# A new order of the same operations in a bucketed attention and token-mixing kernel

## The chip, the cores and the metric

The kernel runs on one core of one Trainium2 chip. The metric is the device time of one execution in microseconds; several executions are timed and the median is given. The core has five engines that take instructions in order, each from its own list: TensorE (PE, matrix products), VectorE (DVE), ScalarE (ACT, functions by tables), GpSimd (POOL), and SyncE (SP), which here issues the DMAs. They wait for one another by semaphores.

## The reference

Two parts follow each other for each of four batches. The first is attention with 8 heads, 768 positions and 64 dimensions, in which a query sees only the keys with the same six sign bits; the second works on the heads' outputs laid side by side (768 x 512).

```python
q_bits, k_bits = (q @ proj > 0), (k @ proj > 0)          # 6 bits, one bucket number each
mask   = q_bucket[:, :, :, None] == k_bucket[:, :, None, :]
scores = np.where(mask, scale * q @ k.T, -1e9)
attn   = exp(scores - max) / sum                         # per row
x      = (attn @ v) laid out as (B, S, H * D)

theta  = x @ w_theta                                     # 768x512 by 512x512
zr, zi = x * cos(theta), x * sin(theta)
u      = x + w_tok_r @ zr + w_tok_i @ zi                 # token mixing, 768x768 weights
out    = u + maximum(u @ w_ch, 0)
```

## The kernel before

**Attention, per head.** q and k are split into a high and a low 16-bit part (`hl`, L573 and L577), their sign bits are computed by a small product (`pb`, L627) and written beside them into the stacked operands `qt` and `kt` (copies of L646, else DMAs). A product `sq` gives scores from which DVE takes row maxima (`mc`, L721); these become a row of `qt`. Then the score product `st` is made again, transposed and with the maximum in it, ACT takes the exponential (`pf`, L799), ACT rounds it to 16 bits (`p1`, L805), POOL computes the rest (`p2`, L811; the profile shows both as `p`), and PE multiplies both with the split values (`po`, `pv` in the list), twice 65 and 64 columns. `vsc` and `vv` (L359 to L362, L490) scale and split the values. A normalisation (L849, L855) writes x.

**The second part, per batch and tile of 128 positions.** A transpose `pt_x` is split into `h_x` (ACT, L905) and `l_x` (DVE, L909); twelve matmuls make `ps_th` (one "theta tile"); ACT and DVE bring the angle to whole turns (`n` L941, `z` L944, its magnitude L950 on ACT or L947 on DVE). For tiles 0 to 2 together, and for 3 to 5, ACT takes sine and cosine (L966, L967), which need another table than exp: a table load stands ahead of them, and another ahead of the next `pf`. DVE makes `f` = x times sine or cosine (L978), which is split into a high half `zh` (L983 on ACT, L985 on DVE) and a low half `zl` (L989, POOL or DVE). Token mixing `py` is 36 matmuls for each output tile; then `u` (DVE, L1017), a transpose `pt_u`, `h_u`, `l_u`, twelve matmuls `ps_r`, `fin` (L1024) and the store. Batch b's second part is interleaved with batch b + 1's attention.

**What sets the order.** All of this is written as a list of operations: `op(name, prio, {engine: (planned duration, function)}, deps, slots, table)`. `prio` is a rank in steps of the attention (96 over the whole kernel) plus constants: `KA` and `KB` for rounding and rest, `PF` for the exponential, `TH0` and `TH1` for theta, `Y0`, `YS`, `Y1` for the mixing, `AS0` for assembling the operands, with variants for the first and last batch (`TH0_3`). `issue_all` runs a plan with planned durations: whenever an engine is free it issues the available operation of the lowest rank, held up by constants (`AHEAD`, `HOLD`, `PEN`, `WIN`). Operations with two engines go to the one that is free first by the plan. The result is a fixed list for each engine; nothing is reordered on the chip. Banks of PSUM come in three pools (`mx` 2, `s` 2 for `st`, `m` 4 for all others), and the matmuls go through a helper, so that all of them show as L78.

Of the kernel before, what the change touches and what calls it, by code (L numbers as in the profile page):

```python
# [34 lines left out]
def lsh_attention_moe_kernel(ctx: ExitStack, tc: tile.TileContext, q, k, v, proj, w_theta, w_tok_r, w_tok_i, w_ch, aff, out):  # L35
# [36 lines left out]
    pst = {}  # L72
# [24 lines left out]

    class Op:
        def __init__(self, name, prio, alts, deps=(), slots=(), table=None):
            self.name, self.prio, self.alts = name, prio, alts  # L100
            self.deps = [d for d in deps if d is not None]
            self.slots, self.table = list(slots), table
            self.phase = phase
            for sl in self.slots:
                sl.users += 1
            ops.append(self)

    ops = []
    phase = "0"
# [5 lines left out]
    def issue_all():  # L115
# [68 lines left out]
        def key(o, e):  # L184
            if e == "PE" and tail_pe in SHORT and o.name in FOUR:
                return (o.key[0] + PEN, o.key[1])
            return o.key
# [28 lines left out]
        while todo:  # L216
            progress = False
            for e in START:
# [3 lines left out]
                for o in avail[e]:  # L222
                    k_ = key(o, e)
                    if best is not None and k_ >= best:
                        continue
                    end = now + (HOLD * o.alts[e][0] if e != "SP" else 0)
                    if any(x.at < end and key(x, e)[0] + AHEAD < k_[0] for x in soon[e]):
                        continue
# [81 lines left out]
    def on(e, dur, fn):  # L310
        return {e: (dur, fn)}
# [28 lines left out]

    cload = op("consts", QKL + 0.03, on("SP", [(625, 0)] * 3, load_consts))
    proj_ready = op("pst", QK0, on("DVE", 700, split_proj), [cload])


    wth = [wp.tile([P, NC, DM], F32R, name=f"wth{i}") for i in range(2)]
# [108 lines left out]
    def prep_v(b, hp, prio):  # L454
# [62 lines left out]

        r = op("vload", prio + LV0, on("SP", [(450, 2 * S * D * 4)], load), slots=[svb])
        r = op("vsq", prio, on("ACT", 900, squares), [r], [svb, sv])
# [27 lines left out]
    def prep_qk(b, hp, G, g):  # L547
# [4 lines left out]
        ssc = t["ssc"] = Slot("sc")  # L552
        pr = G + at("QK0", b)
        for i, src in enumerate((q, k)):
            def part(i=i, src=src):
# [22 lines left out]

                a = op("qkload", G + QKL + 0.02 * i, on("SP", [(625, 2 * S * D * 4)], load), slots=[sn])
                raws.append(a)  # L580
# [25 lines left out]
        for i, sn, high, low in parts:  # L606
            hs.append(op("qkh", pr + QKI * i, pick(g, QKH, {"ACT": (830, high("ACT")), "DVE": (520, high("DVE"))}), [r], [sn, sh, ssc]))
            ls.append(op("qkl", pr + QKI * i, on("DVE", 880, low), [hs[-1]], [sn, sh, ssc]))

# [20 lines left out]

        b1 = op("bits", G + at("QK1", b), on("PE", 1000, bits), raws + [proj_ready], [sm_] + nats)
        direct = []
        if g == 0:
            direct.append(op("sign0", G + at("QK1", b) - 0.01, on("DVE", 4 * 470, first), [b1], [sm_]))
        fs = [op("sign", G + at("QK1", b), on("DVE", 570, sign), [b1], [sm_, sr])]

# [24 lines left out]
    def assemble(j, n_, t, prio, free_after):  # L661
# [12 lines left out]
        def bits():  # L674
# [8 lines left out]
            op("assemble", prio, on("SP", [(1000, 4 * D * n)] * 2 + [(1000, 2 * hd * n)] * 4, parts), t["parts"] + free_after, [sh]),  # L683
            op("assbits", prio + AB, on("SP", [(780, NM * n / 2)] * 4, bits), t["bits"] + free_after, [sr]),
        ]
# [8 lines left out]
    def maxima(h, n_, b, G, asm):  # L694
# [15 lines left out]
        for n, (parts, cs) in enumerate(units):  # L710
            def one(n=n, parts=parts, cs=cs):
# [10 lines left out]

                pr = G + at("MX0", b) + at("MX1", b) * n * T / len(units)
                a = op("qmax", pr, on("PE", 225, scores), asm, [sx])
# [26 lines left out]

        pr = G + at("MX0", b) + at("MX1", b) * T
        a = op("vboth", pr, on("DVE", 90, both), vs, [smc])
# [11 lines left out]
    def step(g, b, h, blk, mxt, vt, piece):  # L765
# [15 lines left out]
        for c in range(nc_):  # L781
            def chunk(c=c):
# [43 lines left out]

                G = g + CL * c * ni / 2
                a = op("st", G, on("PE", 440 + 8 * kc, scores), [mxt["rowd"]], [ss])
                last[n_].append(a)
                i = op("pf", G + PF, on("ACT", 490, pf), [a], [ss, spf], table="exp")  # L830
                d = [done] if done else [mxt["ftd"]] + vt["ready"]
                f = [sft] if c == 0 else []
                k1 = op("p1", G + KA, pick(g, P1, {"ACT": (525, p1("ACT")), "DVE": (337, p1("DVE"))}), [i], [spf, sp1])
                k2 = op("p2", G + KB, pick(g, P2, {"DVE": (610, p2(DVE)), "POOL": (1090, p2(POOL))}), [k1], [spf, sp1, sp2])
                return op("pv", G + KV, on("PE", 385 + 29 * ni * (c == 0), pv), d + [k1, k2], [sp1, sp2, sm_, vt["slot"], sx] + f)

            done = chunk()

        g += (nc_ - 1) * CL * ni / 2
        t["done"] = done  # L840
# [15 lines left out]

        r = op("recip", g + KN, on("DVE", 90, recip), [done], [sm_])
        n = op("norm", g + KN, on("DVE", 135 + 67 * n_, norm), [r], [sm_, sx])
        for i in range(*piece):
# [3 lines left out]
    def moe(b, G):  # L863
# [13 lines left out]

        st0 = op("moe", G + at("TH0", b) - 0.5, on("DVE", 800, start), wready["tk"] + vready[b], sz)

# [52 lines left out]
        for tt in range(T):  # L932
            def theta(tt=tt):
                prio = G + at("TH0", b) + at("TH1", b) * tt
                u, deps, sxt = transposed(lambda: tl[b][:, tt], f"x{b}_{tt}", prio, xready[b][tt // 2], "x")
# [99 lines left out]
    for tau in range(T):  # L1035
        prep_wtok(tau, W0 + WS * tau if tau < LATE else WL0 + WLS * (tau - LATE))
    for c in range(NC):
        split_weight(w_theta, wth, c, (0, DM), "th", "z0", "x", WTH + WTS * c, 1.0 / TWO_PI)
        for half in range(2):
            split_weight(w_ch, wch, c, (half * DM // 2, DM // 2), "ch", "tmp", "tmp", WC + WCS * (c + 0.5 * half))  # L1040
    g = 0
    for b in range(B):
        phase = str(b)
        for hp in range(NP):
            t = prep_qk(b, hp, g, g)
            vt = prep_v(b, hp, g + at("PV0", b))
            order = ORDERS[ORD if b == B - 1 and hp == NP - 1 else 0]
            mxs = []
            for j in range(2):
                n = ((b * NP + hp) * 2 + j) % SETS  # L1050
                free_after, last[n] = last[n], []
                G = g + sum(BLOCKS[k_][1] // 2 for _, k_ in order[: order.index((j, 0))])
                asm = t["first"] if g == 0 and j == 0 else assemble(j, n, t, G + at("AS0", b), free_after)
                mxs.append(maxima(2 * hp + j, n, b, G, asm))
# [3 lines left out]
    for b in range(B):  # L1058
        phase = str(b)
# [7 lines left out]
PSUM = (("mx", 2), ("s", 2), ("m", 4))  # L1067
BUFS = dict(mx=2, s=2, m=4, pf=4, p1=4, p2=4, vb=1, tmp=3)
SETS = 3
CL = 0.331  # L1070
TAIL = ["m", "s"]
ORDERS = [[(0, 0), (0, 1), (1, 0), (1, 1)], [(0, 0), (1, 0), (0, 1), (1, 1)]]
WIN = {"m": 3, "tmp": 3}
MX0 = -3.317
MX1 = 0.379
PIECES = [{1: (0, 3)}, {0: (0, 2), 1: (2, 3)}]
PF = 0.221
KA = 0.466
KB = 0.534
KV = 0.599  # L1080
KN = 1.56
AB = 0.161
WTH = 18.77
WTS = -0.673
WC = 23.047
WCS = 3.231
P1 = [(0, 999, ["ACT"])]
P2 = [(0, 999, ["POOL"])]
GR = 0
PEN = 0.031  # L1090
GR1 = 0
GROUPS = [[(0, 3), (3, 6)], [(0, 4), (4, 6)], [(0, 2), (2, 4), (4, 6)]]
JIT = 0
SEED = 162248
TH0_3 = -0.965
TH1_3 = 0.664
Y0_3 = 2.914
YS_3 = -0.142
Y1_3 = -0.008
MX0_0 = -3.169  # L1100
MX1_0 = 0.368
AS0_0 = -6.248
PV0_0 = -5.09
QK0_0 = -9.684
QK1_0 = -4.644
HOLD = 0.017
LATE = 6
WL0 = 26.724
WLS = -14.449
TH0_0 = 0.111  # L1110
TH1_0 = 0.797
Y0_0 = 9.844
Y1_0 = 1.882
YS_0 = 6.922
AHEAD = 1.647
QKL = -12.399
QKI = 4.506
QKH = [(0, 999, ["ACT", "DVE"])]
QK0 = -6.21
QK1 = -5.177  # L1120
AS0 = 0.585
PV0 = -4.184
LV0 = -2.609
W0 = -0.514
WS = 3.329
TH0 = -0.152
TH1 = 0.823
Y0 = 9.151
YS = 5.605
Y1 = 2.733  # L1130

_INS = ["q", "k", "v", "proj", "moe_w_theta", "moe_w_tok_r", "moe_w_tok_i", "moe_w_ch"]

# [44 lines left out]
```

## Time and profile before

| | |
|---|---|
| runs | 805.57, 806.96, 808.13 us; median 806.96 |
| profiled execution | 808.25 us, of which the span of the trace is 806.1 |
| mean granted clock of TensorE | 0.972 |
| PE, DVE, ACT, POOL busy | 732.8, 547.6, 552.1, 473.9 us |
| `po` (pv), all forms | 154.7 us in 3456 matmuls |
| `py` | 218.2 us in 864 matmuls |

A row of a page's group or a timeline reads: start, busy time, engine, line, operation, output and inputs (partitions x elements, type), count, and in brackets the idle time of the engine ahead of it with what ended it. Slices are fortieths of the span, about 20.15 us each; a digit is the busy share in tenths, and 9 is 90% or more.

### The profile page before, as it was taken

To read this page: it belongs to the slowest core of one execution; us is meant where nothing else is said; L and a number is where in the kernel's file an instruction comes from. 1 tells how busy PE (TensorE), PEld (TensorE's weight loads), DVE (VectorE), ACT (ScalarE), POOL (GpSimd) and SP (SyncE) were. 2 spreads that over 40 slices of the span, in tenths; PEclk is the share of its full clock that TensorE was granted. 3 is DMA by queue.
4 is the path that set the end of the run, shared out by engine and by line. 5 is a ranking of instruction groups with operands and counts; after the bars stand their busy time and mean duration, and the time that the engine had idled before them with its cause. 6 is when DMAs were issued, how large, how long until landed. Compare 5 with 4: busy or idle time off the path is not lost.

```text
span 806.1 us, 17749 instructions
## 1 busy us (share of the span) xinstructions
PE 732.8 (91%) x6760; PEld 472.2 (59%) x6760; DVE 547.6 (68%) x1027; ACT 552.1 (68%) x983; POOL 473.9 (59%) x496
## 2 busy tenths in 40 slices
PE   2578697779899999999899999999899999999998
PEld 1246465447555656767556666668556666675456
DVE  7989999895688746685786655684696755236413
ACT  5488899888787754898887564778796654657101
POOL 4168889687659724695569653765667564631200
PEclk9988999999899999999899999999899999999999
DMA  7354454433103232323003220332004110000002
GB/s 219 87 152 145 135 160 143 130 88 84 38 15 109 66 98 66 98 74 88 27 21 103 80 70 29 101 84 69 21 21 115 46 47 14 15 14 1 1 1 78
DMA packets 35268, 59.52 MB, mean 74 GB/s; under 512 B 7456, under 2 KB 24944, under 8 KB 35184
## 3 DMA queue, kind: packets, MB, share of 16 engines
q1 hardware_dynamic: 35184, 58.40, 25.3%
q8 instruction: 53, 0.87, 0.5%
q14 instruction: 31, 0.25, 0.1%
HBM read 32.51 MB, written 6.29 MB: 48 GB/s over the span
## 4 chain that ended last, share of the span: by engine, by line
PE 69%; DVE 13%; ACT 7%; issue 3%; POOL 3%; DMA 3%; SPq 1%; ACTq 0%; DVEq 0%; POOLq 0%
PE py L78 21%; PE st L78 12%; PE po L78 11%; PE ps_r L78 8%; PE ps_th L78 8%; PE sq L78 5%; DVE mc L721 4%; ACT pf L799 3%; DVE hl L577 1%; POOL p L811 1%; ACT p L805 1%; PE pt_u L900 1%; DVE f L978 1%; PE pt_x L900 1%; PE pb L78 1%
## 5 line engine op out<-in xcount | busy, mean ns | idle before, releaser
L811 POOL TENSOR_TENSOR p<-pf,p 128x512 f16<-128x512 f32 x288 | 365.0, 1290 | 143.3 <-ACT p L805 80.0
L78 PE MATMUL py<-z,wtk 128*128 128x512 f16 x864 | 218.2, 385 | 0.5 <-DVE z L989 0.3
L721 DVE TENSOR_REDUCE mc<-sq 128x1 f32<-128x512 f32 (+1 forms) x288 | 188.8, 681 | 40.8 <-PE sq L78 40.0
L799 ACT ACTIVATE pf<-st 128x512 f32<-128x512 f32 x288 | 163.1, 592 | 75.7 <-PE st L78 66.2
L78 PE MATMUL st<-qt,kt 108*128 108x512 f16 (+3 forms) x768 | 169.9, 338 | 24.7 <-ACT pf L799 23.2
L805 ACT ACTIVATE p<-pf 128x512 f16<-128x512 f32 x288 | 170.8, 628 | 18.2 <-PE po L78 16.8
L78 PEld LDWEIGHTS <-p 128*128 128x128 f16 x3456 | 141.6, 99 | 44.1 <-issue 11.0
L78 PE MATMUL po<-vv,p 128*128 128x65 f16 (+1 forms) x3456 | 154.7, 195 | 3.0 <-POOL p L811 2.4
L78 PEld LDWEIGHTS <-wtk 128*128 128x128 f16 x864 | 82.5, 99 | 85.5 <-issue 9.7
L78 PE MATMUL sq<-kt,qt 108*128 108x256 f16 (+1 forms) x384 | 105.7, 337 | 27.1 <-DVE mc L721 18.2
L78 PEld LDWEIGHTS <-kt 108*128 108x128 f16 (+1 forms) x768 | 72.2, 101 | 74.9 <-issue 42.1
L989 POOL TENSOR_TENSOR z<-f,z 128x512 f16<-128x512 f32 x38 | 50.9, 1348 | 71.2 <-ACT z L983 54.2
L78 PEld LDWEIGHTS <-qt 108*128 108x128 f16 x384 | 35.5, 101 | 51.0 <-issue 30.0
L78 PE MATMUL ps_th<-wth,h_x 128*128 128x512 f32 x192 | 64.2, 416 | 1.2 <-DVE z L944 0.8
L78 PE MATMUL ps_r<-wch,h_u 128*128 128x512 f32 x192 | 63.0, 409 | 0.8 <-DVE l_u L909 0.8
L978 DVE SCALAR_TENSOR_TENSOR f<-x,zsc,z 128x512 f32<-128x512 f32 x48 | 56.2, 1208 | 8.8 <-ACT z L966 4.8
L1017 DVE SCALAR_TENSOR_TENSOR x<-py,sw,x 128x512 f32<-128x512 f32 x24 | 17.9, 746 | 48.7 <-PE py L78 48.7
L1024 DVE SCALAR_TENSOR_TENSOR x<-ps_r,x 128x512 f32<-128x512 f32 x24 | 16.6, 691 | 47.3 <-PE ps_r L78 47.3
L905 ACT ACTIVATE h_u<-pt_u 128x512 fp32r<-128x512 f32 x24 | 14.1, 592 | 50.4 <-PE pt_u L900 33.8
L78 PEld LDWEIGHTS ps_th<-wth,h_x 128*128 128x128 f32 x192 | 36.3, 194 | 10.6 <-DVE z L944 1.3
L78 PEld LDWEIGHTS ps_r<-wch,h_u 128*128 128x128 f32 x192 | 35.0, 188 | 10.5 <-DVE l_u L909 2.4
L577 DVE SCALAR_TENSOR_TENSOR hl<-raw,sc,hl 128x768 f16<-128x768 f32 x32 | 40.2, 1266 | 0.0
(128 smaller groups left out, 904.3 us busy)
## 6 DMA issues: line engine op xcount, KB each, us to landing
raw<-in_q_dram SPq DMA_DIRECT2D x16, 384.0 KB
raw<-in_k_dram SPq DMA_DIRECT2D x16, 384.0 KB
vb<-in_v_dram SPq DMA_DIRECT2D x16, 384.0 KB
out_dram<-x SPq DMA_DIRECT2D x24, 256.0 KB
qt<-hl SPq DMA_DIRECT2D x31, 192.0 KB
kt<-hl SPq DMA_DIRECT2D x31, 192.0 KB
w_t<-in_moe_w_tok_r_dram SPq DMA_DIRECT2D x6, 768.0 KB
w_t<-in_moe_w_tok_i_dram SPq DMA_DIRECT2D x6, 768.0 KB
```

Of the source, the lines that this page charges most:

```text
L78: PE.matmul(out_, l, r, start=start, stop=stop, skip_group_check=True)
L577: DVE.scalar_tensor_tensor(t["hl"][:, 1, i], t["raw", i], t["sc"][:, 2 + i : 3 + i], t["hl"][:, 0, i], ALU.mult, ALU.subtract)
L721: DVE.tensor_reduce(col()[:, cs], u["sq"], AX.X, ALU.max)
L799: ACT.activation(wide("pf", spf, F32), u["st"], AF.Exp, scale=1.0 / (UNIT * math.sqrt(D)))
L805: ACT.activation(o_, u["pf"], AF.Copy)
L811: return lambda: eng.tensor_tensor(wide("p2", sp2, F16), u["pf"], u["p1"], ALU.subtract)
L900: PE.transpose(u["pt"][:, c], src()[:, c * P : (c + 1) * P], ident)
L905: ACT.activation(u["hi"], u["pt"], AF.Copy)
L978: DVE.scalar_tensor_tensor(u["f"], tl[b][:, tt], zsc[:, b : b + 1], t["zw"][r][:, tt], ALU.mult, ALU.mult)
L989: return lambda: eng.tensor_tensor(t["z"][r, 1][:, tt], u["f"], t["z"][r, 0][:, tt], ALU.subtract)
L1017: DVE.scalar_tensor_tensor(tl[b][:, to], res["py"], t["sw"][:, to : to + 1], tl[b][:, to], ALU.mult, ALU.add)
L1024: DVE.scalar_tensor_tensor(tl[b][:, to], r_["ps"], 0.0, tl[b][:, to], ALU.max, ALU.add)
```

## The change

The rank of every operation gets one more term, looked up by kind of operation and batch, and some fifty constants of the ranks and the plan have other values. No operation is added or taken away, and no shape or buffer is changed. The table `OFF` has some 200 entries, of which two rows are shown.

```diff
         def __init__(self, name, prio, alts, deps=(), slots=(), table=None):
-            self.name, self.prio, self.alts = name, prio, alts
+            self.name, self.prio, self.alts = name, prio + OFF.get(name + "/" + phase, 0), alts
...
-CL = 0.331
+CL = 0.323
...
-PF = 0.221
-KA = 0.466
-KB = 0.534
+PF = 0.006
+KA = 0.127
+KB = 1.025
...
-KN = 1.56
+KN = 1.134
...
-PEN = 0.031
+PEN = 1.368
...
-AS0_0 = -6.248
+AS0_0 = -0.017
...
-HOLD = 0.017
+HOLD = 0
...
-AHEAD = 1.647
+AHEAD = 1.118
...
+OFF = {
+    "assbits/0": -1.538, "assbits/1": 0.024, "assbits/2": 7.444, "assbits/3": 0.03, "assemble/0": 0.662, "assemble/2": 2.142,
...
+    "norm/0": 2.061, "norm/1": 3.165, "norm/2": 1.579, "norm/3": -0.278, "p1/0": 0.212, "p1/1": 0.114,
...
```

Where the lists differ is seen at three places. The first is ACT's list in the theta stage of batch 0, from the last magnitude of theta tiles 0 to 2 to the first exponentials behind the sine. In the names the first number after `h_x` or `f` is the batch, the second the tile; in `pf` and `st` they are batch, head, block and chunk. Before:

```order
L950 ACTIVATE z0_0_2864<-z1_0_2865 128x512
L512 ACTIVATE mh_1_1_3213<-pm_1_1_3189,vsc_105 33x128
L513 ACTIVATE mt_1_1_3097<-pm_1_1_3189,vsc_105 1x2x64
L966 ACT_TABLE_LOAD
L966 ACTIVATE z0_0_2864<-z0_0_2864,hpi_84 128x1536
L967 ACTIVATE z1_0_2865<-z1_0_2865 128x1536
L905 ACTIVATE h_x0_4_3273<-pt_x0_4_3208 128x512
L799 ACT_TABLE_LOAD
L799 ACTIVATE pf_1_1_0_0_3283<-st_1_1_0_0_3268 128x512
L799 ACTIVATE pf_1_1_0_1_3294<-st_1_1_0_1_3278 128x512
```

And now:

```order
L905 ACTIVATE h_x0_3_3230<-pt_x0_3_3194 128x512
L966 ACT_TABLE_LOAD
L966 ACTIVATE z0_0_2863<-z0_0_2863,hpi_84 128x1536
L967 ACTIVATE z1_0_2864<-z1_0_2864 128x1536
L390 ACTIVATE wf_ch1_0_3161<-w64_ch1_0_3159 128x256
L391 ACTIVATE wf_ch1_0_3161<-wf_ch1_0_3161 128x256
L905 ACTIVATE h_x0_4_3294<-pt_x0_4_3234 128x512
L983 ACTIVATE z0_0_2863<-f_0_0_0_3288 128x512
L983 ACTIVATE z1_0_2864<-f_0_0_1_3299 128x512
L799 ACT_TABLE_LOAD
L799 ACTIVATE pf_1_1_0_0_3312<-st_1_1_0_0_3284 128x512
```

Two operations on the weights of the last product and two `zh` came between the sine and the reload of exp, and `h_x0_3` came ahead of the sine. On PE, the two `st` that these `pf` read stood ahead of theta tile 4 and right behind `pv`, and now stand behind theta tile 3, with theta tile 4 and six matmuls of `py` between them and the third `st`.

The second place is the same stage of batch 2 on ACT. Before:

```order
L799 ACT_TABLE_LOAD
L799 ACTIVATE pf_3_1_0_0_9085<-st_3_1_0_0_9070 128x512
L799 ACTIVATE pf_3_1_0_1_9096<-st_3_1_0_1_9080 128x512
L805 ACTIVATE p1_3_1_0_0_9104<-pf_3_1_0_0_9085 128x512
L805 ACTIVATE p1_3_1_0_1_9109<-pf_3_1_0_1_9096 128x512
L799 ACTIVATE pf_3_1_0_2_9112<-st_3_1_0_2_9099 128x512
```

And now:

```order
L799 ACT_TABLE_LOAD
L799 ACTIVATE pf_3_1_0_2_9163<-st_3_1_0_2_9093 128x512
L983 ACTIVATE z0_2_8375<-f_2_0_0_9171 128x512
L983 ACTIVATE z1_2_8376<-f_2_0_1_9176 128x512
L983 ACTIVATE z0_2_8375<-f_2_1_0_9179 128x512
L799 ACTIVATE pf_3_1_0_3_9199<-st_3_1_0_3_9157 128x512
```

Chunks 0 and 1 went ahead of the sine, and three `zh`, each of which waits for an `f` of DVE, came between the first and the second `pf` behind the reload.

The third place is DVE's list ahead of the first `sq` of the kernel, from the low parts of the first head on. Before:

```order
L359 TENSOR_SCALAR vsc_105<-pa_0_0_177 128x1
L360 TENSOR_SCALAR vsc_105<-vsc_105 128x1
L361 TENSOR_SCALAR vinv_104<-vsc_105 128x1
L362 TENSOR_SCALAR vsc_105<-vinv_104 128x1
L646 COPY kt0_111<-hl_0_0_139 64x1536
L646 COPY qt0_108<-hl_0_0_139 32x768
L646 COPY kt0_111<-hl_0_0_139 32x768 x2
L627 TENSOR_SCALAR qt0_108<-pb_0_0_160,affs_83 12x384
```

And now:

```order
L627 TENSOR_SCALAR kt0_111<-pb_0_0_160,affs_83 12x384
L646 COPY qt0_108<-hl_0_0_139 32x768
L646 COPY kt0_111<-hl_0_0_139 32x768
L646 COPY qt0_108<-hl_0_0_139 32x768
L646 COPY kt0_111<-hl_0_0_139 32x768
L622 TENSOR_SCALAR rows_0_0_202<-pb_0_0_160,affs_83 128x384
L359 TENSOR_SCALAR vsc_105<-pa_0_0_177 128x1
```

The four sign operations of L627 now come first, the copy of 64x1536 is on ACT, and the `vsc` operations follow the copies and `rows`.

More of the change, by code (lines that the diff above doesn't have):

```diff
@@ L1073 @@
 WIN = {"m": 3, "tmp": 3}
-MX0 = -3.317
-MX1 = 0.379
+MX0 = -3.457
+MX1 = 0.377
 PIECES = [{1: (0, 3)}, {0: (0, 2), 1: (2, 3)}]
-PF = 0.221
-KA = 0.466
-KB = 0.534
+PF = 0.006
+KA = 0.127
+KB = 1.025
 KV = 0.599
-KN = 1.56
[L1082 to L1086, printed above, removed]
+KN = 1.134
+AB = 0.046
+WTH = 20.402
+WTS = -1.556
+WC = 21.845
+WCS = 3.997
 P1 = [(0, 999, ["ACT"])]
@@ L1094 @@
 SEED = 162248
[L1095 to L1101, printed above, removed]
-AS0_0 = -6.248
-PV0_0 = -5.09
-QK0_0 = -9.684
-QK1_0 = -4.644
-HOLD = 0.017
+TH0_3 = -0.218
+TH1_3 = 0.568
+Y0_3 = 7.395
+YS_3 = 1.64
+Y1_3 = -0.193
+MX0_0 = -3.093
+MX1_0 = 0.321
+AS0_0 = -0.017
+PV0_0 = -4.592
+QK0_0 = -10.109
+QK1_0 = -4.891
+HOLD = 0
 LATE = 6
@@ L1109 @@
 WLS = -14.449
[L1110 to L1114, printed above, removed]
-AHEAD = 1.647
-QKL = -12.399
-QKI = 4.506
-QKH = [(0, 999, ["ACT", "DVE"])]
[L1119 to L1130, printed above, removed]
+TH0_0 = 0.29
+TH1_0 = 0.741
+Y0_0 = 9.653
+Y1_0 = 1.826
+YS_0 = 6.248
+AHEAD = 1.118
+QKL = -12.014
+QKI = 4.217
+QKH = [(0, 999, ["ACT", "DVE"])]
+QK0 = -6.194
+QK1 = -5.45
+AS0 = 0.199
+PV0 = -4.052
+LV0 = -0.029
+W0 = -0.197
+WS = 3.268
+TH0 = -0.064
+TH1 = 0.867
+Y0 = 9.131
+YS = 6.102
+Y1 = 2.616
+OFF = {
[36 rows of a table added]
+}
 _INS = ["q", "k", "v", "proj", "moe_w_theta", "moe_w_tok_r", "moe_w_tok_i", "moe_w_ch"]
```

34 rows, old and new, of the table OFF are left out of this document.

## The prediction

> **What bounds the kernel now.** I read the page first (busy shares, slices, chain), then windows of 20 us to see which engine limits which stage, then TensorE's idle time by what ended it, and last the timelines of the places where TensorE stands still, with windows cut on the clock's own grid.
>
> ```profile
> PE 732.8 (91%) x6760; PEld 472.2 (59%) x6760; DVE 547.6 (68%) x1027; ACT 552.1 (68%) x983; POOL 473.9 (59%) x496
> PE   2578697779899999999899999999899999999998
> PEclk9988999999899999999899999999899999999999
> PE 69%; DVE 13%; ACT 7%; issue 3%; POOL 3%; DMA 3%; SPq 1%; ACTq 0%; DVEq 0%; POOLq 0%
> ```
>
> TensorE (PE) is busy for 732.8 of 806.1 us, and the chain that ended last runs 69% on it: 73.3 us of idle time is all that order can remove, plus what is lost to the lower clock. The PE row puts most of the idle time into the first ten slices (0 to 200 us). After that nearly every slice is 9, with three 8s at 200, 380 and 560 us in which the clock row dips too, except for the last slice.
>
> ```profile
> 20.00:40.00 20.00, 11.63 (x46) 5.42 (x46) 19.16 (x41) 8.01 (x14) 2.11 (x8) 1.00 0.29 81
> 200.00:220.00 20.00, 17.32 (x120) 11.22 (x119) 14.21 (x22) 16.32 (x25) 11.95 (x12) 0.83 0.19 52
> 380.00:400.00 20.00, 17.53 (x119) 11.69 (x118) 14.52 (x22) 16.75 (x26) 13.22 (x12) 0.83 0.22 52
> 560.00:580.00 20.00, 17.32 (x127) 11.48 (x124) 13.89 (x20) 15.90 (x26) 10.55 (x10) 0.83 0.10 29
> L78 PE MATMUL sq<-kt,qt 108*128 108x512 f16 x58 | 23.8, 429 | 10.9 <-DVE mc L721 9.7 <-DVE sinv L354 0.9
> L78 PE MATMUL st<-qt,kt 108*128 108x256 f16 (+3 forms) x568 | 121.5, 332 | 10.6 <-ACT pf L799 9.3 <-DMA qt<-row 1.3
> L78 PE MATMUL py<-z,wtk 128*128 128x512 f16 x864 | 218.2, 385 | 0.5 <-DVE z L989 0.3 <-POOL z L989 0.2
> ```
>
> In a windows row the busy times are PE, PE's weight loads, DVE, ACT, POOL, then the granted clock. The start is bound by VectorE (DVE): 19.16 of 20 us. The last three rows are PE groups, the first of 18 to 184 us, the others of 184 to 800 us: early PE waits for DVE's maxima, later nearly only for the exponentials `pf`, 9.3 us in all; the token mixing `py` waits for 0.5 us in 218.2. Those 9.3 us lie mostly at three places, one in each theta stage of batches 0 to 2:
>
> ```profile
> 199.69 0.39 PE L78 MATMUL ps_th<-wth,l_x 128*128 128x512 f32 x1
> 202.53 0.71 PE L78 MATMUL ps_th<-wth,h_x 128*128 128x512 f32 x2
> 203.31 0.63 PE L78 MATMUL ps_th<-wth,h_x 128*128 128x512 f32 x2
> 205.43 0.91 PE L78 MATMUL po<-vv,p 128*128 128x65 f16 x24
> 206.18 1.03 PE L78 MATMUL st<-qt,kt 108*128 108x512 f16 x4
> 207.05 0.60 PE L78 MATMUL sq<-kt,qt 108*128 108x512 f16 x3
> 209.40 1.08 PE L78 MATMUL st<-qt,kt 108*128 108x512 f16 x4 [1.75 <-ACT pf L799]
> 211.41 1.87 PE L78 MATMUL st<-qt,kt 108*128 108x256 f16 x8 [0.93 <-ACT pf L799]
> 390.97 1.29 PE L78 MATMUL st<-qt,kt 108*128 108x512 f16 x4 [1.75 <-ACT pf L799]
> 392.98 1.86 PE L78 MATMUL st<-qt,kt 108*128 108x256 f16 x8 [0.72 <-ACT pf L799]
> 568.19 1.08 PE L78 MATMUL st<-qt,kt 108*128 108x512 f16 x4 [1.75 <-ACT pf L799]
> 570.20 1.86 PE L78 MATMUL st<-qt,kt 108*128 108x256 f16 x8 [0.93 <-ACT pf L799]
> ```
>
> ScalarE's (ACT's) timeline of batch 0 tells why: the sine tables for tiles 0 to 2 and the reload of exp keep every `pf` away, and the two `st` banks stay full.
>
> ```profile
> 202.71 1.28 ACT L966 ACT_TABLE_LOAD   x1
> 204.00 1.58 ACT L966 ACTIVATE z<-z,hpi 128x1536 f32<-128x1536 f32 x1
> 205.49 1.46 ACT L967 ACTIVATE z<-z 128x1536 f32<-128x1536 f32 x1
> 206.86 0.58 ACT L905 ACTIVATE h_x<-pt_x 128x512 fp32r<-128x512 f32 x1
> 207.46 1.28 ACT L799 ACT_TABLE_LOAD   x1
> 208.75 1.08 ACT L799 ACTIVATE pf<-st 128x512 f32<-128x512 f32 x2
> ```
>
> No `pf` starts between 202.71 and 208.75, and the next `st` starts 0.65 us after that `pf` does. PE has run dry by 207.65. The price is not the idle time alone:
>
> ```profile
> 207.36:210.77 3.41, 1.37 (x7) 0.49 (x6) 3.41 (x6) 3.38 (x7) 1.74 (x2) 1.00 0.01 3
> 210.77:214.18 3.41, 2.77 (x11) 1.61 (x11) 2.36 (x4) 3.41 (x8) 2.76 (x3) 0.50 0.00 0
> 214.18:217.60 3.42, 3.42 (x11) 1.78 (x10) 2.12 (x2) 1.13 (x3) 2.53 (x2) 0.50 0.00 0
> 388.26:391.68 3.42, 1.67 (x10) 0.71 (x9) 3.42 (x6) 3.39 (x6) 1.08 (x1) 1.00 0.02 6
> 565.75:569.17 3.42, 1.67 (x9) 0.68 (x7) 3.42 (x6) 3.39 (x6) 1.35 (x2) 1.00 0.03 9
> 159.57:162.99 3.42, 2.03 (x20) 0.91 (x17) 3.07 (x6) 3.39 (x7) 3.34 (x5) 1.00 0.59 134
> ```
>
> In this trace the granted clock changes only on a grid of 3.41 us, and is 1.00 or 0.50. A window with PE busy for 1.37 or 1.67 us (40 and 49%) is followed by two at half clock; one with 2.03 us (59%) is not. A half window costs half of its busy time: 2.77/2 + 3.42/2 = 3.1 us. So a theta stall costs its idle time and 3.1: 5.8, 5.6 and 5.8 us, together 17.2 us.
>
> Here the Trainium skill ("TensorE: Matmul & The Clock Gate", HAM oscillation) speaks against me: it allows idle gaps up to some 3.4 us before the clock drops. The longest gap in these places is 1.75 us and the clock did drop, so row and page differ on the threshold; on the grid and the two levels they agree.
>
> **The change, part by part.** The counts of PE's and SP's instructions stay as they are. A few operations that may run on either of two engines change sides: three or so low halves of z (L989) go from POOL to DVE, four high halves from ACT to DVE. By this trace's means that is about 5 us more of DVE and as much less of ACT and POOL over the whole span; behind PE's 9s it is covered, and in the start it would show one to one, but the largest move there, kt's copy, goes from DVE to ACT. I take nothing for it.
>
> *Theta, batch 0.* From the end of theta tile 2 (199.69 + 0.39, about 200.0) PE had 7.7 us of work before it ran dry. In the new order this joins ahead of the first `st` that needs a `pf`: theta tile 4 (2.9 us, as from 202.53 to 205.43), two `sq` (0.4, as two of the three at 207.05), six `py` (6 × 218.2/864 = 1.5) and a group of four transposes (0.5, an estimate by the `sq`); twelve of `pv` go (0.4, half of the 205.43 to 206.18). That is 12.6 us. On ACT the new order puts `h_x0_3` ahead of the sine, and two weight operations and two `zh` ahead of exp's reload: 0.6 us by the row of `h_x`, and by estimates from it 0.35 for each of the narrower weight operations and 0.6 for each `zh`. So `pf` begins some 11.2 us after tile 2 instead of 8.75. 11.2 + 0.65 is less than 12.6, so that `st` no longer waits. What is late next is theta tile 4, whose `h_x0_4` now stands behind the weight operations: I get 1.1 us of idle time there and 0.9 behind the first `pf`, too far apart for one window, so each window is at least 68% busy. So 5.8 becomes 2.0: −3.8.
>
> *Theta, batch 1.* The cover grows from 7.3 to 8.7 us (theta tile 3 goes behind the `st` banks, more `pv` and `sq` ahead); ACT gets `mh` and `mt` between sine and reload (0.4 us), and the `pf` comes 9.1 us after tile 2. Idle 9.1 + 0.65 − 8.7, about 1.0, and 0.8 behind it: 1.8 within some 3.1 us of time. A window that holds all of it is 47% busy, one that holds only the first part 70%: the clock may go either way. −3.8 with it, −0.7 without.
>
> *Theta, batch 2.* Two `st` banks and their `pf` come ahead of the sine, and theta tiles 1 to 5 are cut into pieces with `pv`, `sq` and `st` between. But three `zh` that need DVE's `f` stand ahead of the second `pf` after the reload. I step it to 1.3 and 0.5 us of idle time: 5.8 becomes 1.8, −4.0 with the clock kept, −0.9 without.
>
> All three kept: −11.6. The phase of the grid against the program decides, and I cannot know it; the likeliest is that one of three is lost: −11.6 + 3.1 = −8.5.
>
> *Start.*
>
> ```profile
> 16.55 1.01 PE L78 MATMUL sq<-kt,qt 108*128 108x512 f16 x2 [7.19 <-DVE kt L627]
> 11.52 0.15 DVE L359 TENSOR_SCALAR vsc<-pa 128x1 f32<-128x1 f32 x1
> 12.15 0.54 DVE L646 COPY kt<-hl 64x1536 f16<-64x1536 f16 x1
> ```
>
> Four `vsc` operations (11.52 to 12.15) go behind the copies, and the copy of 0.54 us goes to ACT: signs and copies end 0.63 + 0.54 earlier, less one copy of 0.35 that DVE takes over for `qt` (an estimate, two thirds of the 0.54): about −0.8 for the first `sq`. Behind that DVE is the bound until 180 us, and its order is shuffled: the row maxima of heads 0 to 7 come with 0.6 us less to 1.4 us more DVE work ahead of them. Bounds: −4 (two of its half windows fewer) to +4; I take the −0.8 that a row shows.
>
> *Price of cutting.* A theta or `ps_r` run's first pair takes 0.71 us instead of 0.63: 0.08 per entry, ten more entries, mostly in batch 2: +0.8. *New small waits* in the token mixing, where PE is at 9s: the 0.5 us of `py` can't fall by more, and the whole of what `st` has beside its three theta stalls is 10.6 − 7.8 = 2.8; bounds −2 to +4 (a wait like that in each of batches 0 to 2), and near the lower row I take +1. *End.* All theta tiles of batch 3 come ahead of its mixing, the sine earlier; PE is already full there: −0.5, bounds −1.5 to +1.
>
> Sum: −8.5 − 0.8 + 0.8 + 1.0 − 0.5 = −8.0. The profiled execution took 808.25 us (span 806.1), 1.3 over the median of 806.96; on the median's scale the forecast is 799.0.
>
> **The rivals.**
>
> *All three keep the clock:* −11.1, 795.9. For it: idle times of 1.8 to 2.0 us, split over two windows, against 2.5 to 2.7 in one. Against: batch 1's 47%.
>
> *The clock is lost as before, only idle time goes.* 7.8 us of idle time become 5.6: −2.2, with +0.5 of the rest −1.7: 805.3, within 0.3%. By the page's rule, too, gaps of 1.75 us cost no clock, so filling them would bring this and no more; the rows at 210.77 and 388.26 speak against it. Between this and the forecast lies one batch kept, 802.1.
>
> *Slower:* ACT runs in order, and the new order puts `zh` ahead of exp's reload (batch 0) or of a `pf` (batch 2). If DVE comes to `f` late, every `pf` comes late by as much.
>
> ```profile
> 565.93 1.40 DVE L978 SCALAR_TENSOR_TENSOR f<-x,zsc,z 128x512 f32<-128x512 f32 x2
> 567.92 3.20 DVE L978 SCALAR_TENSOR_TENSOR f<-x,zsc,z 128x512 f32<-128x512 f32 x2
> ```
>
> Two `f` took 1.40 us, the next two 3.20, so 2 us late is possible. Then each of the two stalls costs 2.0 + 2 + 3.1 = 7.1 against 5.8 (+2.6), batch 1 stays, the rest +0.5: +3.1, 810.1. It decides from 0.7 us late on, where these stalls cost what they cost now.
>
> **How the numbers follow.** Two batches kept 0.40 (its own range 795 to 803, by start and small waits), all three 0.25, one 0.12, none 0.08, slower 0.15. A difference under 0.3% (2.4 us) can't be told from none. With the start's ±4 about each, faster 0.70, same 0.14, slower 0.16. The range 792.5 (all three and a start 3.4 us shorter) to 808.5 leaves out half of the slower case and the far end of the best.
>
> **What would show it.** Windows on the 3.41-us grid around the theta stages of batches 0 to 2 with no 0.50; the first `st` behind the reload without 1.75 us of idle time; in batch 0 idle time at `ps_th` released by `h_x` or `l_x` instead; first `sq` near 15.75 us; DVE still at 19 of 20 us up to 180. I am wrong if half windows stay in the theta stages, if `pf` is released late by `f`, or if the start's half windows grow in number.

## The result and the profile after

The new order takes 786.18 us (median of four runs, 786.01 to 786.79), the kernel before 806.66 (805.57 to 808.13): a ratio of 0.9746 with an interval of 0.9729 to 0.9763, so 2.5% or 20.5 us faster. Forecast were 799.0 us and a range that ended at 792.5. The profiled execution took 786.11 us, its span 784.3.

The page of the new kernel, the same rows as of before:

```profile
PE 721.0 (92%) x6760; PEld 468.2 (60%) x6760; DVE 558.1 (71%) x1033; ACT 547.2 (70%) x979; POOL 473.3 (60%) x494
PE   2578897779999999999999999999999999999997
PEclk9989799999999999999999999999999999999999
```

The three 8s at 200, 380 and 560 us are gone, and so are their dips of the clock. Busy time fell by 11.8 us with the same matmuls: PE was busy at half clock for 39.6 us before and for 22.3 now, and half of that difference, 8.7 us, is lost time that went. Idle time fell from 73.3 to 63.3.

Two TensorE (PE) groups of 184 to 800 us:

```profile
L78 PE MATMUL st<-qt,kt 98*128 98x256 f16 (+3 forms) x558 | 120.0, 326 | 2.8 <-ACT pf L799 2.5
L78 PE MATMUL py<-z,wtk 128*128 128x512 f16 x864 | 210.7, 379 | 0.0
```

And PE's timeline at the places in the theta stages where it still waits, two in batch 0, two in batch 1, one in batch 2:

```profile
203.70 0.73 PE L78 MATMUL ps_th<-wth,h_x 128*128 128x512 f32 x2 [0.18 <-ACT h_x L905]
210.48 0.60 PE L78 MATMUL st<-qt,kt 108*128 108x256 f16 x4 [0.40 <-ACT pf L799]
371.58 0.38 PE L78 MATMUL sq<-kt,qt 108*128 108x512 f16 x1 [0.32 <-DVE mc L721]
380.33 1.09 PE L78 MATMUL st<-qt,kt 108*128 108x256 f16 x8 [0.46 <-ACT pf L799]
560.41 0.59 PE L78 MATMUL st<-qt,kt 108*128 108x512 f16 x2 [0.95 <-ACT pf L799]
```

The wait of `st` for `pf` fell from 9.3 to 2.5 us. With two more of 0.18 and 0.17 us the three stages hold 0.58, 0.96 and 1.12 us of idle time. The sparsest windows on the clock's grid in these stages (busy times of PE, PE's weight loads, DVE, ACT, POOL, then the clock):

```profile
209.68:213.10 3.42, 3.02 (x30) 1.90 (x29) 3.32 (x4) 3.39 (x7) 3.42 (x4) 1.00 0.00 0
376.94:380.35 3.41, 2.91 (x14) 1.55 (x13) 3.38 (x5) 3.40 (x7) 2.50 (x2) 1.00 0.46 131
557.84:561.26 3.42, 2.47 (x17) 1.51 (x16) 3.42 (x4) 3.42 (x7) 2.09 (x3) 1.00 0.00 0
```

They are 88, 85 and 72% busy, against 40 to 49% before, and no window behind 185 us is at half clock until PE has ended. ACT's timeline shows why `pf` is no longer missed:

```profile
204.70 1.28 ACT L799 ACT_TABLE_LOAD   x1
206.00 1.09 ACT L799 ACTIVATE pf<-st 128x512 f32<-128x512 f32 x2
```

Theta tile 2 ends at 195.5, so `pf` begins 10.5 us after it, later than before (8.75); PE has other work until 210.1.

To see where the time went, I gave each matmul the usual distance between starts of its form at full clock (0.22 us for 512 columns of 16 bits, 0.235 for one of theta), added them up in order, and noted when each kernel had done equal work. The whole is 671.6 us of such work. (In the text below, "at equal work" is this reckoning.)

| work done | what ends there | before | new | difference | of this stretch |
|---|---|---|---|---|---|
| 100 | the start | 188.8 | 184.1 | −4.7 | −4.7 |
| 200 | batch 0's second part, nearly | 298.8 | 287.9 | −10.9 | −6.2 |
| 400 | batch 1's | 514.8 | 499.9 | −14.9 | −4.0 |
| 600 | batch 2's | 728.7 | 708.3 | −20.3 | −5.4 |
| 671.6 | the last matmul | 802.3 | 779.9 | −22.4 | −2.1 |

Behind the last matmul the new kernel needs 0.6 us more, hence 21.8 on the span.

### The profile page after: what moved, and what is told of

It is laid out like the page before. It is cut to its first block, busy times and chain, and to the rows that moved or that the text cites. A ratio compares the mean times of both kernels' runs of the same rounds, so it can differ in the third digit from the quotient of the medians.

```text
span 784.3 us, 17811 instructions
## 1 busy us (share of the span) xinstructions
PE 721.0 (92%) x6760; PEld 468.2 (60%) x6760; DVE 558.1 (71%) x1033; ACT 547.2 (70%) x979; POOL 473.3 (60%) x494
## 4 chain that ended last, share of the span: by engine, by line
PE 48%; ACT 4%; DVE 2%; issue 1%; DMA 0%; POOL 0%; ACTq 0%; SPq 0%; DVEq 0%
PE py L78 16%; PE st L78 7%; PE ps_r L78 7%; PE po L78 6%; PE ps_th L78 6%; PE sq L78 3%; PE pt_u L900 1%; ACT pf L799 1%; PE pt_x L900 1%; DVE mc L721 0%; ACT n L941 0%; PE pb L78 0%; ACT z L966 0%; ACT z L967 0%; ACT p L805 0%
## 5 line engine op out<-in xcount | busy, mean ns | idle before, releaser
L78 PE MATMUL py<-z,wtk 128*128 128x512 f16 x864 | 210.7, 379 | 0.0
L805 ACT ACTIVATE p<-pf 128x512 f16<-128x512 f32 x288 | 172.8, 630 | 10.3 <-PE po L78 8.1
L989 POOL TENSOR_TENSOR z<-f,z 128x512 f16<-128x512 f32 x34 | 47.6, 1410 | 46.1 <-ACT z L983 32.1
L978 DVE SCALAR_TENSOR_TENSOR f<-x,zsc,z 128x512 f32<-128x512 f32 x48 | 58.6, 1257 | 3.6 <-ACT z L966 2.5
```

What stands on the lines that cost most here:

```text
L78: PE.matmul(out_, l, r, start=start, stop=stop, skip_group_check=True)
L805: ACT.activation(o_, u["pf"], AF.Copy)
L978: DVE.scalar_tensor_tensor(u["f"], tl[b][:, tt], zsc[:, b : b + 1], t["zw"][r][:, tt], ALU.mult, ALU.mult)
L989: return lambda: eng.tensor_tensor(t["z"][r, 1][:, tt], u["f"], t["z"][r, 0][:, tt], ALU.subtract)
```

## The experiments

The two orders are permutations of the same 3863 operations, and as lists they stay close: cut after 940 operations (where batch 0's theta begins), each has issued the same operations, four of them on another engine. So most experiments follow one list up to a cut and the other from there on, leaving out what is already issued. `issue_all` then issues from a list instead of planning:

```diff
-        for o in sorted(ops, key=lambda o: o.key):
-            run(o)
-...
+        for n, e, idxs in LIST:
+            late.append((ops[n], e, idxs))
+            ...
```

In the kernels the lists stand packed; `LIST` below is a short form that says which order holds up to which operation.

The kernel before ran beside each set; its medians there were 804.1, 804.2, 805.4 and 804.4 us, with single runs from 799.4 to 810.5. Over all 95 of these the median is 804.55, so the 806.66 of the four runs above lies high, and against 804.55 the new kernel's 786.18 is 18.4 us faster rather than 20.5. A gain in us below is the ratio's distance from 1 times the median beside it; the ratio differs from that of the two medians by 0.1 to 0.2% in some sets.

**The start alone.**

```diff
+LIST = NEW[:940] + [x for x in BEFORE if x not in NEW[:940]]
```

> The list of operations follows the new order for its first 940 operations (up to the first theta transpose of batch 0) and the order before from there on; the two orders have then issued the same set but for two operations. Theory (the gain is a sum over stages, and the start's share is what the two traces show when equal TensorE work is lined up, 4.7 us): about 802 us, ratio 0.994. Rival (the start is bound by VectorE and its gain is lost in the first theta stall, which waits for the tables anyway): 805 to 808, no difference. Rival (the start's share is chance of the clock grid): the ratio moves by more than 0.5% between runs.

Measured: 801.77 us, ratio 0.9959 (0.9937 to 0.9982), 3.3 us. At equal work its start is 6.0 us shorter, so the start's share is real. But its trace loses 4.6 us again at 362 us, where before had waited for 0.84 us. PE's timeline in this run, then ACT's, then ACT's in the kernel before:

```profile
362.73 1.01 PE L78 MATMUL st<-qt,kt 108*128 108x256 f16 x4 [3.48 <-ACT pf L799]
```

```profile
361.26 0.84 ACT L566 ACTIVATE hl<-raw 128x768 f16<-128x768 f32 x1 [4.20 <-DMA qt<-hl]
```

```profile
365.57 0.84 ACT L566 ACTIVATE hl<-raw 128x768 f16<-128x768 f32 x1 [1.56 <-DMA raw<-in_q_dram]
```

ACT stands at `hl`, which needs q's load; the load was issued at 354.19 and used 7.1 us later, before at 361.15 and 4.4 us later. ACT's row in this run names `qt<-hl` as what ended the wait, but the landings on the semaphore of q's load tell more: 15 of its 16 parts had landed by 357.27 and the last at 360.72, in the kernel before by 364.24 and at 365.31. With the same lists there, a load that comes 2.7 us late stops every `pf` behind it, and two windows at half clock follow (361.1 to 367.9 us). One execution shows it; it can be a source of the spread of this order.

**The three theta stretches alone.**

```diff
+LIST: BEFORE to 940, NEW to 1125, BEFORE to 1987, NEW to 2098, BEFORE to 2804, NEW to 3026, BEFORE to the end
```

> The order before, with the new order in three stretches alone: operations 940 to 1125, 1987 to 2098 and 2804 to 3026 of the list, the theta stages of batches 0 to 2. Theory (each stall costs its idle time and two windows at half clock, and both go): 17.2 us less some 2 us of idle time left, so about 792 us, ratio 0.981, with no half-clock window behind 190 us. Rival (the gain of batch 0 to 2 lies as much in the token mixing between, where the new order waits less): 797 to 800. Rival (only the idle time goes, the clock drops for another reason): 801 to 803.

Measured: 802.96 us, ratio 0.9971 (0.9946 to 0.9995): 2.3 us and a miss. At equal work batch 0's stage gained 5.2 us, batch 1's 2.9, batch 2's 4.0; and then 6.0 were lost. This run's timelines of PE and of ACT:

```profile
588.17 1.01 PE L78 MATMUL st<-qt,kt 108*128 108x512 f16 x2 [4.07 <-ACT pf L799]
```

```profile
584.02 0.63 ACT L983 ACTIVATE z<-f 128x512 f16<-128x512 f32 x1 [0.37 <-DVE f L978]
585.58 0.63 ACT L983 ACTIVATE z<-f 128x512 f16<-128x512 f32 x1 [0.93 <-DVE f L978]
586.23 1.28 ACT L799 ACT_TABLE_LOAD   x1
587.52 1.09 ACT L799 ACTIVATE pf<-st 128x512 f32<-128x512 f32 x2
```

The last cut fell into the sine of tiles 3 to 5, and what the list before has next, three `zh` ahead of exp's reload, met DVE late. That is the mechanism of my slower rival, with its price: 4.07 us of idle time and two windows at half clock. It did not happen in the new order, where the first three `f` of batch 2 came in time, but it is real.

**Idle time filled, not shortened.** The kernel before in its own order, with matmuls that add zeros to the last `sq` bank ahead of each stall:

```diff
+                    if nm in WARM and n == 5:
+                        for _ in range(WARM[nm]):
+                            mm(sq.rearrange("p x n -> p (x n)"), zer[:K1], kt[:K1, 0, 0:512], False, True)
+WARM = {"1_2": 8, "2_2": 8, "3_2": 8}
```

> The kernel before, in its own order, with eight matmuls by a zero weight added to the last sq bank ahead of each of the three theta stalls (1.7 us of work that adds zeros, so the idle time of 1.75 us is filled and not shortened). Theory (the half-clock windows come from PE standing still in the window before them, whatever the work): the six half-clock windows behind 200 us go, 9.1 us, less up to 1 us by which the added work delays something: 797 to 799 us, ratio 0.989. Rival (gaps under 3.4 us cost no clock; the half windows have another cause, such as the kind of work): 807 to 809, with the same half-clock windows.

Measured: 798.68 us (797.62 to 800.86), ratio 0.9920 (0.9889 to 0.9951), 6.4 us, though PE does 24 matmuls more. PE's timeline in batch 0, and the window on the grid:

```profile
206.81 1.89 PE L80 MATMUL sq<-kt,zer 108*128 108x512 f16 x8
208.73 1.08 PE L80 MATMUL st<-qt,kt 108*128 108x512 f16 x4
210.74 1.09 PE L80 MATMUL st<-qt,kt 108*128 108x256 f16 x8 [0.93 <-ACT pf L804]
```

```profile
207.36:210.77 3.41, 2.46 (x12) 0.90 (x10) 3.41 (x5) 3.40 (x7) 2.41 (x2) 1.00 0.01 2
```

The next `st` takes 1.08 us as before and starts no earlier than its `pf` allows, but the window is 72% busy and the two behind it run at full clock; in this trace none of the six half windows behind 200 us is left, and its last matmul ends 8.8 us earlier. So standing still does cost the clock here, in gaps of 1.75 us. On the median the gain is smaller than the trace's. Most other executions of the kernel before lose fewer windows than the profiled one, whose mean granted clock was 0.972: over the 95 executions that clock lay between 0.967 and 0.985, which is 16 to 7 half windows (twice the share that is missing from 1, times the span, over 3.41 us), and the time rose as it fell (correlation −0.77). With the zeros it was 0.980 to 0.987.

With two such matmuls instead of eight:

> As with eight, with two such matmuls: 0.44 us of added work ahead of each stall. The windows that were 40 to 49% busy come to 53 to 62% if the grid stands as it did. Theory (the clock is lost below some share between 49 and 54 to 59% of a window): most of the half-clock windows go in most executions, 798 to 803 us, and the spread over executions is wider than with eight since the grid's phase decides. Rival (a longest gap decides, 1.3 us still being too long): 806 to 808.

Measured: 802.14 us (798.65 to 806.46), ratio 0.9958 (0.9934 to 0.9982); in the trace one half window each in batches 0 and 1 and none in batch 2, as the theory had it, and the spread, 7.8 us over 12 runs, is more than twice that of eight (3.2 over 6).

**The middle, one batch of it, and the two ends.**

```diff
+LIST: BEFORE to 940, NEW to 3652, BEFORE to the end          (the middle)
+LIST: BEFORE to 940, NEW to 1786, BEFORE to the end          (batch 0 alone)
+LIST: NEW to 940, BEFORE to 3652, NEW to the end             (the ends)
```

> The order before for the first 940 operations and from operation 3652 on (the last batch's second part), the new order between, where both have issued the same set to within a few operations. Theory (the stages add up as the traces line up): −15.3 us against the kernel before, ratio 0.981, and no half-clock window behind 190 us. Rival (the theta stages gain only if the start has the new order too): less than half of that, ratio over 0.990.

Measured: 792.58 us, ratio 0.9843 (0.9815 to 0.9870), 12.6 us; at equal work its middle is 15 to 16 us shorter, and the clock of its page has dips in the start alone:

```profile
PEclk9988899999999999999999999999999999999999
```

> The new order for operations 940 to 1786 alone, from the first theta transpose of batch 0 to a place ahead of batch 1's theta stage where both orders differ by one operation. Theory: −6.1 us, ratio 0.9925; the theta stage of batch 0 without half-clock windows, those of batches 1 and 2 as before. Rival (a splice costs more than a stage brings, as with the three theta stretches alone): 0.997 to 1.003.

Measured: 799.96 us, ratio 0.9937 (0.9913 to 0.9961), 5.1 us; in the trace the half windows of batch 0 are gone, two each in batches 1 and 2 are there.

> The new order for the first 940 operations and from operation 3652 on, the order before between. Theory: −4.7 and −2.4, so −7.1 us, ratio 0.991, with the half-clock windows of the theta stages still there. Rival (the end gains nothing, since PE is full there): −4.7, ratio 0.994.

Measured: 800.47 us, ratio 0.9946 (0.9919 to 0.9973), 4.3 us, and two half windows in each theta stage. At equal work its end gains 2.1 us, as in the new kernel.

The middle and the ends add up to 12.6 + 4.3 = 16.9 us, against 18.4 to 20.5 of the whole, which is within the two intervals. The middle carries 60 to 75% of the gain, by which of these it is measured.

**Constants and table apart.**

```diff
-OFF = { ... }
+OFF = {}
```

> The new constants with an empty table of offsets, so the plan is made anew. Theory (what matters is where the operations stand at the few stalls, and any change of a rank moves them): the gain does not split into constants and table; somewhere between 800 and 830 us, with half-clock windows at theta stages again. Rival (the constants bring the gain and the table is trimming): 786 to 792.

> The constants of the kernel before with the new table of offsets, planned anew. Theory (table and constants are one fitted set; half of it gives an order that nobody fitted): slower than before, 810 to 840 us, as the constants alone were. Rival (the table brings the gain by itself): 786 to 795.

Measured: the new constants without the table 822.78 us, ratio 1.0209 (1.0174 to 1.0245); the constants before with the new table 854.62, ratio 1.0615 (1.0580 to 1.0650). Either half of the set is slower than both kernels, and the half windows of the first spread over the whole start (14) and three places behind it. Neither the constants nor the table hold the gain by themselves; only the order that comes of both does.

**What bounds the start.**

The kernel before with POOL's part of batch 0's attention cut short:

```diff
+                    if b == 0:
+                        return lambda: eng.tensor_tensor(wide("p2", sp2, F16)[:, :32], u["pf"][:, :32], u["p1"][:, :32], ALU.subtract)
```

> The kernel before with POOL's rounding rest p2 of batch 0's attention cut to 32 of 512 columns; pv multiplies a tile of zeros in its place (same matmuls, and one more of 65 columns per chunk that reads the short p2). Left out: batch 0's low parts. Theory (part of the start's gain is that VectorE's two-input operations meet POOL less often: hl L577 took 1.43 us on average in the start before and 1.24 after, and single ones 1.91 beside POOL and 1.01 without): L577, L385 and L394 get shorter by a quarter, and the first theta stage starts 5 to 12 us earlier. Rival (VectorE's operations last as long as they last, and its time was set by what it waits for): no shorter L577, and the start changes by under 2 us.

Measured: 802.84 us, ratio 0.9982 (0.9958 to 1.0006), and theta began at 188.9 us as before, although VectorE (DVE) worked 14 us less. It settled nothing: the matmul of 32 weights that was to read the short p2 went with some 13 us more busy time on PE. So it was tried again without that matmul:

> The kernel before with POOL's p2 of batch 0's attention cut to 32 of 512 columns, which nothing reads any more; pv multiplies zeros in place of it, in the same number of matmuls (left out: batch 0's low parts, and pv's wait for POOL). Theory (VectorE's time bounds the start): L577 and L394 15 to 25% shorter, 10 us or more of VectorE time less, and the first theta stage at least 5 us earlier. Rival (a chain over PE, VectorE and ACT bounds it, of which VectorE's two-input operations are no part): VectorE's time falls by as much and the first theta stage moves by under 2.5 us, of which pv's wait for POOL is 1.8.

Measured: 798.41 us, ratio 0.9921 (0.9886 to 0.9956), and theta began at 181.3 us, 7.4 earlier. DVE's `hl` group in the start and the busy times of 20 to 184 us, first of the kernel before and then of this one (its line numbers are two higher):

```profile
L577 DVE SCALAR_TENSOR_TENSOR hl<-raw,sc,hl 128x768 f16<-128x768 f32 x10 | 14.2, 1432 | 0.0
```

```profile
20.00:184.00 164.00, 124.43 (x1351) 79.46 (x1351) 151.05 (x277) 135.64 (x248) 120.39 (x115) 0.93 0.43 130
```

```profile
L579 DVE SCALAR_TENSOR_TENSOR hl<-raw,sc,hl 128x768 f16<-128x768 f32 x10 | 10.4, 1048 | 0.0
```

```profile
20.00:184.00 164.00, 125.82 (x1444) 82.08 (x1444) 140.55 (x284) 141.82 (x263) 51.18 (x120) 0.96 0.44 135
```

With POOL's work cut from 120 to 51 us, the same ten `hl` take 1048 ns instead of 1432, and the start is shorter. That speaks for DVE's time as a bound, longer beside a busy POOL; but 10.5 us less of DVE work gave 7.4, `pv`'s wait for POOL went too, and the first try, with 14 us less of DVE work and 13 more of PE, gave nothing. So DVE is not the only bound.

Then the new order in one part of the start at a time:

```diff
+LIST: NEW to 187, BEFORE to the end                          (to 46 us)
+LIST: BEFORE to 187, NEW to 376, BEFORE to the end           (46 to 80 us)
+LIST: BEFORE to 376, NEW to 940, BEFORE to the end           (80 to 184 us)
```

> The new order for the first 187 operations alone (to about 46 us). Theory (the signs and copies that come first are what counts, as forecast): the first sq near 15.2 instead of 16.55 us, the first theta stage (188.8 us in the trace before, 187 to 190 over the runs with the old start) 1 to 1.4 us earlier. Rival (the early gain grows along the start): 3 to 5 us earlier.

> The new order for operations 187 to 376 alone (46 to 80 us). Theory (row maxima of heads 2 and 3 came 2 to 3 us earlier there on equal heads): the third row of maxima near 67.5 instead of 70.3 us, and the first theta stage 2 to 3 us earlier. Rival (it is taken back later in the start): under 1 us.

> The new order for operations 376 to 940 alone (80 to 184 us). Theory: the remaining 1 to 1.5 us. Rival (most of the gain comes here, heads 5 to 8): 3 us or more.

The first theta matmul in the kernel before, in the new one, and in these three runs:

```profile
188.78 0.71 PE L78 MATMUL ps_th<-wth,h_x 128*128 128x512 f32 x2
```

```profile
184.24 0.71 PE L78 MATMUL ps_th<-wth,h_x 128*128 128x512 f32 x2
```

```profile
187.90 0.71 PE L78 MATMUL ps_th<-wth,h_x 128*128 128x512 f32 x2
```

```profile
183.62 0.71 PE L78 MATMUL ps_th<-wth,h_x 128*128 128x512 f32 x2
```

```profile
184.64 0.71 PE L78 MATMUL ps_th<-wth,h_x 128*128 128x512 f32 x2
```

Ratios: 1.0015 (0.9988 to 1.0042), 0.9956 (0.9927 to 0.9986) and 0.9975 (0.9940 to 1.0010). The first 46 us bring nothing that lasts, while either of the other two parts brings the whole 4 to 5 us by itself, more than I had expected of each; together they don't bring twice that. Over the runs with the start of before, theta began at 187.0 to 189.9 us, so 1 to 2 us of each figure may be chance.

The clock is not what shortened the start: both orders have seven half windows there. The windows from 20 us to the first theta matmul, of the kernel before and of the new one, and the new one's `hl` in that stretch:

```profile
20.00:188.78 168.78, 129.08 (x1433) 83.58 (x1433) 154.16 (x283) 140.26 (x257) 125.17 (x119) 0.93 0.44 131
```

```profile
20.00:184.24 164.24, 127.52 (x1437) 84.26 (x1436) 152.16 (x286) 140.46 (x259) 125.11 (x121) 0.93 0.44 134
L577 DVE SCALAR_TENSOR_TENSOR hl<-raw,sc,hl 128x768 f16<-128x768 f32 x10 | 12.3, 1237 | 0.0
```

DVE is busy for 2.0 us less, as much as the ten `hl` take less (1237 ns instead of 1432), and stands idle for 2.5 us less. So both a faster and a better filled DVE are in the 4.5 us; which moves in the order brought them about stays open.

**Two tries at a faster one.** Zeros behind each `pv` chunk of batch 0 in the new kernel, and the new order with batch 1's mixing from before:

```diff
+                    if b == 0:
+                        for _ in range(2):
+                            mm(t["acc"].rearrange("p t w -> p (t w)"), zer[:, :P], zer[:, : T * W1], False, True)
```

> The new kernel with two matmuls by zeros (390 columns, 0.17 us each) behind each of the 72 pv chunks of batch 0, 24 us of added PE work in the start, where PE stands still for some 50 us and 7 half-clock windows lie. Theory (the start is bound by VectorE, so a faster PE helps only where PE ends a wait): the half-clock windows of the start fall to 0 to 3, and the time changes by −5 to +3 us, ratio 0.994 to 1.004 of the new kernel's 786. Rival (the 11 us lost to the clock there are on the path): −8 to −11.

Measured: 788.52 us, ratio to the kernel before 0.9795 (0.9766 to 0.9824). The page's clock row has no dip left that a digit shows:

```profile
PEclk9999999999999999999999999999999999999999
```

The half windows of the start fell from 7 to 2, and the time did not fall: theta began at 186.4 us, 2.2 later than in the new kernel. So most of the 11 us of work that PE loses to half clock in the start is not on the path, or is paid back by the 24 us of added work; the run doesn't tell which.

```diff
+LIST: NEW to 2206, BEFORE to 2506, NEW to the end
```

> The new order except for operations 2206 to 2506 (token mixing of batch 1), which follow the order before, because there the new order waits 1.1 us for l_u ahead of a ps_r and loses 1.3 us against the order before on equal work. Theory (stages add): 784.9, 1.3 us under the new kernel, below what can be told with certainty. Rival (the splice brings a wait of its own, as in the run with three stretches): 787 to 792.

Measured: 786.57 us (785.14 to 788.86), ratio 0.9773 (0.9746 to 0.9800). No gain: at equal work the 1.3 us were won near 445 us, and 1.8 were lost ahead of that, behind the first cut. The new order stays the fastest kernel measured.

## Why the prediction was wrong, point by point

The direction and the mechanism of the theta stalls held. What failed is the sum: the terms for what the new order leaves and adds were each too small a gain or too large a cost, the start's most of all. It was too small by 14 us on the profiled executions (12.8 on the medians), and the range by 6. The signs that I had named came, among them a first `sq` at 15.17 us, no half window in the theta stages and seven in the start as before; but "DVE at 19 of 20 us up to 180" took one window for the whole start, where the windows of 20 us read 17.3 to 19.3 before and 17.4 to 19.6 now.

- **The bound.** Right: what order could remove lay in three theta stalls and in the start, and the three stalls carried most of it. The middle alone gave 12.6 of 18.4 to 20.5 us.
- **The price of a stall,** idle time and two half windows: right in the trace, 5.6 to 5.8 us each, and shown by filling the gap with zeros. But it is not the price of every execution. Runs with the theta order of before had from one (the third part of the start) to six half windows behind 185 us: more or less of the same stall falls into one grid window. I had put the phase down as a risk of the new order, and it was one of the old.
- **The term mis-sized first: the idle time left.** I stepped 2.0, 1.8 and 1.8 us, and the trace has 0.58, 0.96 and 1.12: 2.9 us. In batch 0 theta tile 4 waits 0.18 us for `h_x` where I had 1.1: the `pf` came 10.5 us after tile 2, not 11.2, and the cover reached to 210.1. My stepping charged each operation's full duration on ACT and overstated what stood ahead.
- **The chosen case: one of three batches loses the clock.** None did, 3.1 us. The rival with all three kept (0.25) was the case, but its 795.9 is still 9.7 too high, so the case was not the main error. My 47% for batch 1's window was 85%, since its waits (0.32, 0.18 and 0.46 us) end at 371.6, 374.2 and 380.3 us instead of within 3.1 us of each other.
- **The start: −0.8 forecast, −4.7 in the trace,** the largest error. I costed what I could count, the first `sq`: 15.17 us where I had 15.75. That is not where it came from: the part to 46 us alone gave nothing that can be told from chance. The gain came from 46 to 184 us, which I had noted only as "shuffled", with bounds of ±4 and no value: DVE's busy time fell by 2.0 us there and its idle time by 2.5.
- **Price of cutting (+0.8) and new small waits (+1.0):** together they came out at −1.1: the middle gained 15.6 us at equal work, and the stalls are 17.2 − 2.7 = 14.5 of it. `ps_th` and `ps_r` together are as busy as before. New small waits did come, 1.4 us of the transposes `pt_x` for `l_x`, 0.5 more of `pv` for POOL and 0.3 more of `ps_r` for `l_u`, but more went, which I had only put into the bounds (`py`, `ps_th`, `st` for its row of maxima): all waits behind 184 us other than those for `pf` fell from 5.7 to 5.0 us.
- **The end: −0.5 forecast, −2.1 at equal work.** Before had four waits there (0.39 us on `h_x`, 0.18, 0.34 and 0.84 on `z`), the new kernel none behind 709 us, though 0.21 and 1.23 us for `l_x` just ahead of it. I had called PE "already full" from a digit 9, which hides up to 10% of 20 us.
- **The slower rival** did not come, but the run with three theta stretches showed its mechanism once, at 6.0 us.

Added up: 2.9 + 3.1 + 3.9 + 1.6, and 2.9 for the two charges (+1.8 forecast, −1.1 measured), is 14.4 us, which brings −8.0 to the −22.4 of the last matmul. All these errors lie on one side: unknowns were charged as costs or at nothing, and no gain was taken beyond what a row showed.

## What to carry to other kernels

Price a stall of the busiest engine with what the clock does after it, and fill it with any useful work before trying to shorten it. Where a stage is a chain over several engines and an order moves all of it, line up equal work rather than single rows, and give the unknown part a value from its bounds on both sides instead of only costs. A digit 9 of a slice row is no proof that an engine is full: four short waits hid in it.

## What the runs showed of the hardware

I fitted the grid of 3.41 us to the clock's changes in all 18 traces and counted windows between 30 and 770 us by PE's busy share and the clock of the window behind them:

| window at full clock, PE busy | windows | next at half clock |
|---|---|---|
| under 51% | 103 | 97 |
| 51 to 57% | 39 | 17 |
| 57 to 63% | 61 | 11 |
| 63 to 70% | 75 | 2 |
| over 70% | 3432 | 0 |

| window at half clock, PE busy | windows | next at half clock again |
|---|---|---|
| under 80% | 43 | 43 |
| 80 to 90% | 20 | 15 |
| 90 to 96% | 19 | 5 |
| over 96% | 108 | 0 |

So the clock is lost mostly by share, between about one half and two thirds, and comes back only behind a window that is over 80% busy, in all 108 cases behind one over 96%. The longest gap inside the window tells less: one limit on the share (53%) puts 31 of these windows on the wrong side, the best limit on the gap (1.6 us) 70; a window whose longest gap was 0.47 us lost the clock, and one with 1.8 us kept it. Neither tells it exactly. The Trainium skill ("TensorE: Matmul & The Clock Gate", What's actually happening) has a free-running window of 3413 ns, which these traces show, and a drop after an idle window, which they don't: half-busy windows were enough.

DVE's two-input `hl` took 1432 ns on average beside a busy POOL and 1048 ns when POOL had little to do. And one of the 16 parts of a load landed 3.5 us behind the other 15 in one execution and 1.1 us behind them in another; ACT, which takes its list in order, stood at the load's first reader, and PE waited for 3.48 us.
